# Linear attention and a gated feed-forward layer on one core: four more units and half a block in seven products, one more set turned by TensorE, a new opening

## The chip, the cores and the metric

The kernel runs on one core of one Trainium2 chip. The metric is the device time of one execution in microseconds, the median over several runs. Engines are named as in the profile: PE is TensorE (PEld its weight loads), DVE is VectorE, ACT is ScalarE, POOL is GpSimd, SP is SyncE, which here only issues DMAs.

## The reference

Attention with a decay for each head, in blocks of 64 positions, for 4 batches, 8 heads, 768 positions and 64 features; then a two-layer network with SiLU over 3072 tokens, 512 wide, 2048 inside. Inputs and outputs are float32.

```python
Dmask = np.where(rel >= 0, lam[:, None, None] ** rel[None, :, :], 0.0)      # rel = i - j in a block
lam_pow = lam[:, None, None] ** (pos[None, :, None] + 1)
for b in range(nb):
    qb, kb, vb = (q[:, :, sl], k[:, :, sl], v[:, :, sl])
    intra = np.einsum('bhic,bhjc->bhij', qb, kb) * Dmask[None]
    intra = np.einsum('bhij,bhjd->bhid', intra, vb)
    inter = np.einsum('bhid,bhde->bhie', qb * lam_pow[None], kv_state)
    out[:, :, sl] = intra + inter
    kb_dec = kb * lam[:, None, None] ** (block - 1 - pos[None, :, None])
    kv_state = lam_block[None, :, None, None] * kv_state + np.einsum('bhsd,bhse->bhde', kb_dec, vb)
x = attn_out.transpose(0, 2, 1, 3).reshape(3072, 512)
h = x @ w_in                     # 512 x 2048
out = (h / (1 + np.exp(-h))) @ w_out   # 2048 x 512
```

## The kernel before

**Units, sets, groups.** A unit is 128 positions of one batch, (n, b), with n = 0 to 5 and b = 0 to 3: 24 units, numbered in the order in which they are finished. The attention is done for sets of two units: sets 0 to 3 are blocks 0 and 1 of one batch each (units 0 to 7, "paired", functions `prepare_2`, `first_2`, `second_2`), sets 4 to 11 are two batches of one block n = 2 to 5. Each set loads q, k and v with SP's queue, casts and scales them to bf16 (`kq`, `vd`), turns k and q (`kqT`), makes scores (`st_ps`), masks them on DVE (`st`), makes the state's increment (`d_ps`), the new state (`xf`, and as blocks `xe` in bf16) and the output x, which is copied as `xt`. Sets below `TURNED` (5) are turned by PE transposes with four copies out of PSUM, the others by one DMA transpose on SP's queue.

**The first product.** Its tokens come in groups: groups 0 to 3 are the paired sets (256 tokens), groups 4 to 7 the blocks n = 2 to 5 (512 tokens; "block 4" is n = 4, group 6). `product1` multiplies w_in by xt in plain matmuls (four for each of the 16 rows of features, L905) and ACT applies SiLU to give g (L917). The last group goes through `product1_spared`: h is taken as a 2 x 2 matrix of blocks, and each of four passes `jp` makes four feature rows with seven block products (L1023, 28 matmuls of 256 columns in place of 16 of 512). It needs four sums of w_in (`S1` to `S4`, `sums_of_w_in`), four of xt (`T1` to `T4`), copies of partial results (`keep`) and sums (`total_of`).

**The second product.** `product2_plain` handles one unit with 16 matmuls of 512 columns (L940). Units from number `PLAIN` (8) on go four at a time through `product2`: seven products of 16 matmuls of 256 columns (L1153), with sums of g made by DVE (16 for four units, written as `s` or over `g`), sums of w_out (`sums_of_w_out`, the last over w_out itself once all plain units are done), kept products (`m`) and results added on DVE (`osb`). The last four units are done in two halves.

**The order.** Nothing is issued in the order of the program text. Each step is a task with a key (its rank), costs by engine, what it depends on, and the buffers that it takes; class `Planner` runs through time with these costs, a model of the DMA queues (`SMALL`, `LARGE` and so on, `FIRST`, `LAST`) and a slower PE at the start (`SLOW`), gives each engine the ready task with the lowest key, chooses the engine where there are several, and writes out the order. On the chip each engine then runs its list in that order. A task's key in the set's steps is `s`, which is the unit's rank less a lead, plus or minus a little. Early on, the planner puts PE matmuls without use ("ones", L1236) where PE would be idle.

The loads of the opening follow `SEQUENCE`: set 0, w_in's first part once set 0's v has landed, set 1, and so on; "s2@1.2" holds set 2's loads on SP until set 1's v has landed, by a small DMA that reads it (`held`, L439).

Of the kernel before, what the change touches and what calls it, by code (L numbers as in the profile page):

```python
# [216 lines left out]
def kernel(  # L217
# [27 lines left out]
    FRESH, TURNED, ALONE, LEAD = 4, 5, 6, 6.5  # L245
# [3 lines left out]
    BY_POOL, IN_BY_POOL, PLAIN, SPARED = (), (), 8, 1  # L249
# [4 lines left out]
    SCORED, SOON, VD_ON, HALVED = (0, 1), 3, {"DVE": 0.7}, 0  # L254
    EAGER, CALM, ON = 8.0, 1.0, 6.0
# [94 lines left out]


# [16 lines left out]
    def load_set(key, si):  # L368
        n, b = sets[si][0]
        nb = 2  # L370
        rs = [Buf("rb") if si >= CASTING and i == 0 else None if si >= CASTING and i == 1 else Buf("ra" if si in (0, 3) else "rb")
              for i in range(3)]
        ts = []
        x = [t[b, :, 0:2 * U, :].rearrange("h (p e) d -> p h (e d)", e=2) if n < PAIRED else
             t[b:b + 2, :, n * U:n * U + U, :].rearrange("b h s d -> s (b h) d") for t in (k, q, v)]

        def go(e, i):
            if n < PAIRED:
                tile_of(rs[i], [128, H, 2, 64], F32, "raw")
                nc.sync.dma_start(out=rs[i].tile.rearrange("p h e d -> p h (e d)"), in_=x[i])  # L380
            elif si >= CASTING and i < 2:
                tl = tile_of(rs[0], [128, 2, 2, NP, 2, 64], BF16, "kq")
                nc.gpsimd.dma_start(out=tl[:, i].rearrange("p b m h d -> p (b m h) d"), in_=x[i])
            else:
                nc.sync.dma_start(out=tile_of(rs[i], [128, 2 * H, 64], F32, "raw"), in_=x[i])

        for i in (1, 0, 2) if si in QUERIES else range(3):
            if si >= CASTING and i < 2:
                t = pool_task(add((key, i), {"POOL": 0.8}, lambda e, i=i: go(e, i), bufs=[rs[0]], nbytes=0.524, kind=CAST,
                                  prior=pool_last[-1:] + raw[si - 1][1][2], late=2.0))  # L390
                ts.append([t])
# [10 lines left out]
    def load_w(key, what, j, part):  # L402
        def go(e):
# [3 lines left out]
            else:  # L407
# [4 lines left out]
                          HALF if part else LARGE, prior=pool_last[-1:], late=1.0))  # L412
# [7 lines left out]
    for m, x in enumerate(SEQUENCE.split() + [f"s{i}" for i in range(len(sets))]):  # L420
# [59 lines left out]
    def prepare_2(o, rs, lk, lq, lv):  # L480
# [5 lines left out]
        def cast(e, i, a):  # L486
            src = rs[i].tile[:, :, a, :].rearrange("p (m h) d -> p m h d", h=2)
            if i:
# [5 lines left out]
        o.ck = [[add((s - (2.95 if i and o.si in SCALED else 1.0), i), {"DVE": 0.7} if i else {"DVE": 0.45, "ACT": 0.63}, lambda e, i=i, a=a: cast(e, i, a),  # L494
# [28 lines left out]
    def first_2(o):  # L523
# [26 lines left out]
        def blocks(xe, i, src, t, buf):  # L550
# [5 lines left out]
            return [add((s - 0.9, 5), {"POOL": 0.5, "ACT": 0.42}, lambda e, r=r: go(e, r), deps=[t], bufs=[xe, buf])  # L556
# [9 lines left out]
        def rest():  # L566
# [6 lines left out]
            t2 = add((s - 0.9, 5), {"DVE": 0.42}, lambda e: tt(e, xf_of(), y.tile, rate, AL.mult), deps=[t1], bufs=[y, xf_n])  # L573
# [5 lines left out]
        deps = [t for t in o.turned]  # L579
        o.masked = []  # L580
        for g in range(2):
# [9 lines left out]
            ts = add((s - 0.5, g), {"PE": 0.4}, scores, deps=deps, bufs=st_ps[g] + [o.kqT])  # L591
# [42 lines left out]
    def prepare(si):  # L634
# [28 lines left out]
        def cast(e, j, i):  # L663
            src = rs[i].tile[:, j * H:j * H + H, :]
            dst = kq_of()[:, i, j].rearrange("p m h d -> p (m h) d")
            if i:
# [4 lines left out]
        ck = [[add((s - 1.0, i), {"DVE": 0.7} if i else {"DVE": 0.45, "ACT": 0.63}, lambda e, j=j, i=i: cast(e, j, i),  # L671
# [4 lines left out]
        def scale_v(e, j):  # L676
            tt(e, vd_of()[:, j], rs[2].tile[:, j * H:j * H + H, :], lam_v[:, :, None].to_broadcast([128, H, 64]), AL.mult)

        cv = [add((s - 0.8, 0), VD_ON, lambda e, j=j: scale_v(e, j),
# [114 lines left out]
    def after_first(o, t):  # L794
# [20 lines left out]
        def blocks(b, src, deps, bufs, i):  # L815
# [6 lines left out]
            return [add((s - 0.9, i), {"POOL": 0.25 + w / 1000, "ACT": 0.2 + w / 1200, "DVE": 0.1 + w / 1900}, lambda e, r=r: go(e, r),  # L822
# [65 lines left out]
    def product1(gi):  # L888
# [5 lines left out]
        for m0 in range(0, KO, 2 * per):  # L894
# [69 lines left out]
    def sums_of_w_in():  # L964
        bufs = {name: Buf("kq") if i else Buf("rb") for i, name in enumerate(("S1", "S2", "S3", "S4"))}
# [4 lines left out]

        every = [t for o in infos if rank[o.n, o.bs[0]] < SUMS_AFTER for t in o.cv] + [t for o in infos[:CASTING] for ts in o.ck for t in ts]

        def total(name, a, b, op, deps, on):
            done[name] = [add((on, 8), {"POOL": 2.4} if name in IN_BY_POOL else {"DVE": 0.7}, lambda e, ks=ks: tt(
                e, W[name]()[:, ks], W[a]()[:, ks], W[b]()[:, ks], op), deps=deps, bufs=[bufs[name]])
# [9 lines left out]
    def product1_spared(gi, wbufs, wdone):  # L985
# [5 lines left out]
        def X(name):  # L991
            i, r = {"B11": (0, lo), "B12": (0, hi), "B21": (1, lo), "B22": (1, hi), "T1": (0, hi)}.get(name, (0, lo))
            if name in ("T2", "T4"):
                return tile_of(two, [128, 2, 2, 256], BF16, "xsum")[:, int(name == "T4")]
            if name == "T3":
                return tile_of(one, [128, 2, 256], BF16, "xsum")
# [9 lines left out]
        total("T1", "B12", "B11", AL.subtract, done["T3"], [])  # L1006
        total("T4", "B21", "T2", AL.subtract, done["T2"], [two])
        for jp in range(4):
            P, R = Buf("bank"), Buf("bank")
            held = [P, R, Buf("sp")]  # L1010
# [24 lines left out]
            narrow = {"22": Buf("vd"), "12": Buf("st")}  # L1035
# [175 lines left out]
    for gi in range(len(groups) - SPARED):  # L1211
        product1(gi)
# [4 lines left out]
    if SPARED:  # L1217
        made = sums_of_w_in()
        for gi in range(len(groups) - SPARED, len(groups)):
            product1_spared(gi, *made)  # L1220
# [52 lines left out]
```

## Time and profile before

| | us |
|---|---|
| median of 3 runs (lowest, highest) | 204.46 (204.32, 205.02) |
| the profiled execution: its time | 204.46 |
| its span in the trace | 202.4 |
| mean granted PE clock | 0.997 |
| busy: PE, DVE, ACT, POOL | 188.1, 135.5, 114.2, 21.8 |

DMA engines are at 9 tenths or more from the second to the 27th of the 40 slices of the span; 27.27 MB are read from HBM and 6.29 MB written. An engine's row in the slices gives its busy share in tenths. In the groups of instructions, "x16 | 7.2, 447" means sixteen of them, 7.2 us busy, 447 ns each.

### The profile page before, as it was taken

How to read it: one execution, taken by the hardware profiler on the slowest of the kernel's cores; microseconds unless marked ns; L12 is line 12 of the kernel's file. 1: busy time of each engine (PE TensorE's matmuls, PEld its weight loads, DVE VectorE, ACT ScalarE, POOL GpSimd, SP SyncE). 2: the span in 40 equal slices, each digit the busy share in tenths (PEclk: the TensorE clock that was granted, in tenths of full speed). 3: DMA queues.
4: the chain of work that ended last, by engine and by line, in shares of the span. 5: the costliest groups of instructions: out<-in, count | busy, mean ns of one | idle time of the engine just before them, and what ended most of it. 6: DMA issues, size and time to landing. Idle time of an engine off the chain costs nothing.

```text
span 202.4 us, 5779 instructions
## 1 busy us (share of the span) xinstructions
PE 188.1 (93%) x2494; PEld 135.0 (67%) x2512; DVE 135.5 (67%) x269; ACT 114.2 (56%) x207; POOL 21.8 (11%) x48
## 2 busy tenths in 40 slices
PE   0588999999999999999999999999999999999992
PEld 0476788557678655544488746486676778888881
DVE  6499620595997950969999774999577553646511
ACT  3836666327567642357764394945656575685320
POOL 6093100310110100001011000110200000000000
PEclk9999999999999999999999999999999999999998
DMA  3999999999999989999999999948001111003313
GB/s 94 301 274 202 216 215 250 254 193 212 239 269 242 206 204 261 174 267 212 202 142 231 253 194 222 225 104 160 2 3 55 52 52 36 19 0 107 104 50 108
DMA packets 87067, 33.40 MB, mean 165 GB/s; under 512 B 65026, under 2 KB 86018, under 8 KB 87042
## 3 DMA queue, kind: packets, MB, share of 16 engines
q1 hardware_dynamic: 77154, 23.07, 57.0%
q0 software_dynamic: 4752, 4.19, 12.9%
q10 hardware_dynamic: 5136, 5.77, 8.9%
q8 instruction: 19, 0.31, 0.7%
q14 instruction: 6, 0.05, 0.1%
HBM read 27.27 MB, written 6.29 MB: 166 GB/s over the span
## 4 chain that ended last, share of the span: by engine, by line
PE 84%; DVE 6%; DMA 4%; ACT 3%; issue 1%; DVEq 0%; SPq 0%
PE h_ps L905 33%; PE o_ps L1153 22%; PE o_ps L940 14%; PE h_ps L1023 6%; DMA raw<-in_k_dram 3%; DVE st L349 2%; PE x_ps L767 2%; PE d_ps L727 1%; PE tr L513 1%; PE x_ps L759 1%; DVE vd L349 1%; PE st_ps L737 1%; DMA out_dram<-osb 1%; ACT xt L342 1%; DVE kqT L344 1%
## 5 line engine op out<-in xcount | busy, mean ns | idle before, releaser
L905 PE MATMUL h_ps<-xt,w_in_bf 128*128 128x256 bf16 (+1 forms) x440 | 73.7, 317 | 0.7 <-ACT xt L342 0.3
L905 PEld LDWEIGHTS <-w_in_bf 128*128 128x128 bf16 x448 | 42.9, 98 | 24.9 <-issue 0.3
L917 ACT ACTIVATE g<-h_ps 128x512 bf16<-128x512 f32 x80 | 46.8, 595 | 20.9 <-PE h_ps L905 20.3
L940 PE MATMUL o_ps<-w_out_bf,g 128*128 128x512 bf16 x118 | 28.6, 379 | 0.8 <-issue 0.5
L1153 PEld LDWEIGHTS <-g 128*128 128x128 bf16 x256 | 25.0, 98 | 3.7
L349 DVE TENSOR_TENSOR st<-st_ps,tri 128x512 bf16<-128x512 f32 x32 | 20.3, 682 | 9.3 <-PE st_ps L737 9.3
L1153 PEld LDWEIGHTS <-s 128*128 128x128 bf16 x192 | 18.7, 98 | 2.8
L349 DVE TENSOR_TENSOR kq<-raw,lam_q 128x512 bf16<-128x512 f32 x24 | 16.3, 698 | 6.2 <-DMA raw<-in_q_dram 4.5
L940 PEld LDWEIGHTS <-g 128*128 128x128 bf16 x128 | 12.0, 98 | 12.0
L349 DVE TENSOR_TENSOR osb<-o_ps,m 128x512 f32<-128x512 f32 (+1 forms) x15 | 8.6, 581 | 13.4 <-ACT m L342 8.6
L342 ACT ACTIVATE xt<-x_ps 128x512 bf16<-128x512 f32 x16 | 9.7, 631 | 12.3 <-PE x_ps L767 9.2
L349 DVE TENSOR_TENSOR vd<-raw,lam_v 128x512 bf16<-128x512 f32 x24 | 15.7, 682 | 0.7 <-DMA raw<-in_v_dram 0.7
L1153 PE MATMUL o_ps<-w_out_bf,s 128*128 128x256 bf16 x128 | 15.3, 273 | 0.0
L1153 PE MATMUL o_ps<-wsum,g 128*128 128x256 bf16 x128 | 15.1, 273 | 0.0
L1153 PE MATMUL o_ps<-w_out_bf,g 128*128 128x256 bf16 x128 | 14.8, 273 | 0.0
L342 ACT ACTIVATE osb<-o_ps 128x512 f32<-128x512 f32 (+1 forms) x13 | 7.3, 564 | 12.7 <-PE o_ps L940 8.6
L349 DVE TENSOR_TENSOR s<-g 128x512 bf16<-128x512 bf16 x16 | 7.2, 447 | 10.8 <-ACT g L917 8.1
L342 ACT ACTIVATE m<-o_ps 128x512 f32<-128x512 f32 (+1 forms) x13 | 6.7, 515 | 13.1 <-PE o_ps L1153 12.9
L513 PE MATMUL tr<-ident,kq 128*128 128x128 bf16 x64 | 6.1, 241 | 7.7 <-DVE kq L349 7.5
L342 ACT ACTIVATE kq<-raw 128x512 bf16<-128x512 f32 x14 | 8.4, 624 | 4.5 <-DMA raw<-in_k_dram 4.0
L346 POOL CAST xe<-xf 64x256 bf16<-64x256 f32 (+1 forms) x8 | 5.1, 640 | 49.4 <-DVE xf L349 39.3
L513 PEld LDWEIGHTS <-kq 128*128 128x128 bf16 x64 | 4.6, 107 | 8.4 <-DVE kq L349 7.9
(90 smaller groups left out, 225.0 us busy)
## 6 DMA issues: line engine op xcount, KB each, us to landing
raw<-in_q_dram SPq DMA_DIRECT2D x12, 512.0 KB, 8.2
raw<-in_k_dram SPq DMA_DIRECT2D x12, 512.0 KB, 7.9
raw<-in_v_dram SPq DMA_DIRECT2D x12, 512.0 KB, 7.2
out_dram<-osb ACTq DMA_DIRECT2D x20, 256.0 KB, 4.2
w_out_bf<-in_moe_w_out_dram POOLq DMA_DIRECT2D x4, 512.0 KB, 14.9
w_in_bf<-in_moe_w_in_dram POOLq DMA_DIRECT2D x3, 512.0 KB, 11.7
w_in_bf<-in_moe_w_in_dram POOLq DMA_DIRECT2D x2, 256.0 KB, 8.2
out_dram<-osb ACTq DMA_DIRECT2D x4, 128.0 KB, 1.7
```

The lines of the kernel that those rows point to most:

```text
L342: nc.scalar.activation(o, i, AF.Copy)
L344: nc.vector.tensor_copy(o, i)
L346: nc.gpsimd.tensor_copy(o, i)
L349: (nc.vector if e == "DVE" else nc.gpsimd).tensor_tensor(o, a, b, op=op)
L513: nc.tensor.transpose(t[:, m, a], o.kq_of()[:, i, m, a], ident)
L727: nc.tensor.matmul(d_of(c)[rp, j, m, :], lhsT=o.kq_of()[r, 0, j, m, p, :], rhs=o.vd_of()[r, j, 2 * m + p, :], start=j == 0 and m == 0, sto ...
L767: nc.tensor.matmul(x_of(c)[:, j, m, :], lhsT=o.xe[c].tile[:, (bs[0] + j) % 2, m, :], rhs=o.kqT_of()[:, 1, j, m, halves[c]], start=False, s ...
L905: nc.tensor.matmul(t[:, j, :], lhsT=w_in_bf[:, ko, 128 * (m1 + j):128 * (m1 + j) + 128], rhs=xt[gi].tile[:, ko, :], start=(ko == 0), stop= ...
L917: nc.scalar.activation(t[:, half * per:half * per + per], bank.tile, AF.Silu)
L940: nc.tensor.matmul(t, lhsT=g.tile[:, j, 128 * gp:128 * gp + 128], rhs=w_out_bf[:, ko, :], start=(ko == 0), stop=(ko == KO - 1))
L1023: nc.tensor.matmul(t[:, j, :], lhsT=W[w]()[:, k2, f:f + 128], rhs=X(r)[:, k2, :], start=first and j == 0 and k2 == 0, stop=True, skip_grou ...
L1153: nc.tensor.matmul(t[:, i_, :], lhsT=src(j)[:, k2, 128 * r:128 * r + 128], rhs=W[w]()[:, 2 * j + k2, :], start=first and i_ == 0 and j == ...
```

## The change

- `PLAIN` 8 to 4: units 4 to 7 leave `product2_plain` and go through `product2`. `ON` 6 to 0: the sums of w_out get an earlier key.
- `MIXED = (0, 1)`: of group 6's four passes, two go through `product1_spared`, two stay in `product1`. Their copies use buffers of other pools (`kq`, `y`, `yf`). The sums of w_in lie in `rb` buffers but for S3, and come once the last load has been issued, no longer after the casts; T1 gets a place of its own.
- `TURNED` 5 to 6: set 5 is turned by PE.
- The held load ahead of set 2 counts 2.2 us in the plan instead of 0.15.
- In the paired sets: scores of one half wait for that half's turned pieces alone (`FINE`), the next state xf has a later key (`LAZY`), and its xe copies may run on ACT or DVE, not on POOL (`XE_2`).
- The planner's figures for DMA kinds and starts change.

```diff
-SMALL, WIDE, CAST, LARGE, HALF, TURN = (256, 17.5, 20.0), (512, 25.0, 28.0), (256, 14.0, 31.0), (2048, 88.0, 90.0), (1024, 58.0, 58.0), (1024, 50.0, 50.0)
+SMALL, WIDE, CAST, LARGE, HALF, TURN, PART = (256, 17.5, 20.0), (512, 25.0, 28.0), (256, 14.0, 31.0), (2048, 86.0, 86.0), (1024, 58.0, 58.0), (1024, 50.0, 50.0), (1024, 45.0, 45.0)
...
-    SLOW, SLOWER = 15.5, 1.8
+    SLOW, SLOWER = 14.0, 1.8
-    FIRST, LAST, AHEAD = {"SP": 1.9, "ACT": 1.15, "POOL": 2.5}, 1.0, 0.75
+    FIRST, LAST, AHEAD = {"SP": 1.7, "ACT": 1.15, "POOL": 3.0}, 1.0, 0.75
...
-    FRESH, TURNED, ALONE, LEAD = 4, 5, 6, 6.5
+    FRESH, TURNED, ALONE, LEAD = 4, 6, 6, 6.5
-    BY_POOL, IN_BY_POOL, PLAIN, SPARED = (), (), 8, 1
+    BY_POOL, PLAIN = (), 4
-    SCORED, SOON, VD_ON, HALVED = (0, 1), 3, {"DVE": 0.7}, 0
-    EAGER, CALM, ON = 8.0, 1.0, 6.0
+    SCORED, SOON, HALVED = (0, 1), 3, 0
+    LAZY, FINE, SAFE = 2.0, True, 0.3
+    XE_2, XE_B, XE_P = {"ACT": 0.42, "DVE": 0.35}, 0.1, True
+    MIXED, APART, KEPT = (0, 1), 1, "yf"
+    EAGER, CALM, ON = 8.0, 1.0, 0.0
...
         t = pool_task(add((key, 0), {"POOL": 0.8}, go, [], [], 0.5243 if part else 1.0486,
-                          HALF if part else LARGE, prior=pool_last[-1:], late=1.0))
+                          PART if part else LARGE, prior=pool_last[-1:], late=1.0))
...
-                held = [add((m - 100, -1), {"SP": 0.15}, lambda e, g=gates, tile=tile: nc.sync.dma_start(
+                held = [add((m - 100, -1), {"SP": 2.2}, lambda e, g=gates, tile=tile: nc.sync.dma_start(
...
-            return [add((s - 0.9, 5), {"POOL": 0.5, "ACT": 0.42}, lambda e, r=r: go(e, r), deps=[t], bufs=[xe, buf])
+            return [add((s - 0.9, 5), XE_2, lambda e, r=r: go(e, r), deps=[t], bufs=[xe, buf])
...
-            t2 = add((s - 0.9, 5), {"DVE": 0.42}, lambda e: tt(e, xf_of(), y.tile, rate, AL.mult), deps=[t1], bufs=[y, xf_n])
+            t2 = add((s + LAZY, 5), {"DVE": 0.42}, lambda e: tt(e, xf_of(), y.tile, rate, AL.mult), deps=[t1], bufs=[y, xf_n])
...
-            ts = add((s - 0.5, g), {"PE": 0.4}, scores, deps=deps, bufs=st_ps[g] + [o.kqT])
+            ts = add((s - 0.5, g), {"PE": 0.4}, scores, deps=o.turned[g::2] if FINE else o.turned, bufs=st_ps[g] + [o.kqT])
...
-    def product1(gi):
+    def product1(gi, tiles=None):
...
-        for m0 in range(0, KO, 2 * per):
+        for m0 in tiles or range(0, KO, 2 * per):
...
-        bufs = {name: Buf("kq") if i else Buf("rb") for i, name in enumerate(("S1", "S2", "S3", "S4"))}
+        bufs = {name: Buf("kq" if name == "S3" else "rb") for name in ("S1", "S2", "S3", "S4")}
...
-        every = [t for o in infos if rank[o.n, o.bs[0]] < SUMS_AFTER for t in o.cv] + [t for o in infos[:CASTING] for ts in o.ck for t in ts]
+        issued, casts = [sp_last[-1]], [t for ts in infos[-1].ck for t in ts]
...
-        total("S1", "A21", "A22", AL.add, loads + every, on)
+        total("S1", "A21", "A22", AL.add, loads, on)
-        total("S3", "A11", "A21", AL.subtract, loads + every, on + 0.2)
+        total("S3", "A11", "A21", AL.subtract, casts, on + 0.2)
...
-    def product1_spared(gi, wbufs, wdone):
+    def product1_spared(gi, wbufs, wdone, parts):
...
-        total("T1", "B12", "B11", AL.subtract, done["T3"], [])
+        total("T1", "B12", "B11", AL.subtract, xt_done[gi], [one])
-        for jp in range(4):
+        closing = gi == len(groups) - 1
+        for jp in parts:
...
-            narrow = {"22": Buf("vd"), "12": Buf("st")}
+            narrow = {"22": Buf("vd" if closing else "y"), "12": Buf("st" if closing else "y")}
-            b2, c2 = keep("kqT", [m6])
+            b2, c2 = keep("kqT" if closing else "kq", [m6])
-            b3, c3 = keep("xf", [m7])
+            b3, c3 = keep("xf" if closing else KEPT, [m7])
...
-    for gi in range(len(groups) - SPARED):
+    for gi in range(len(groups) - 2):
         product1(gi)
...
+    made = sums_of_w_in()
+    left = [j for j in range(4) if j not in MIXED]
+    if left:
+        product1(len(groups) - 2, [m for j in left for m in (2 * j, 2 * j + 8)])
+    if MIXED:
+        product1_spared(len(groups) - 2, *made, MIXED)
+    product1_spared(len(groups) - 1, *made, range(4))
```

More of the change, by code (lines that the diff above doesn't have):

```diff
@@ L349, in tt, with by_act, by_rate @@
         (nc.vector if e == "DVE" else nc.gpsimd).tensor_tensor(o, a, b, op=op)
+    def by_act(what, si, a):
+        return {"ACT": 1.7} if f"{what}{si}{a}" in ON_ACT else {"DVE": 0.7}
+    def by_rate(e, o, i, rate):
+        if e == "ACT":
+            nc.scalar.activation(o, i, AF.Copy, scale=rate)
+        else:
+            nc.gpsimd.tensor_scalar(o, i, rate, None, op0=AL.mult)
     gate = const.tile([128, 16], F32, name="gate")
@@ L487, in cast @@
             src = rs[i].tile[:, :, a, :].rearrange("p (m h) d -> p m h d", h=2)
-            if i:
+            if i and e != "DVE":
+                for h in range(H):
+                    by_rate(e, o.kq_of()[:, i, h // 2, a, h % 2], rs[i].tile[:, h, a], lam_q2[:, h, a:a + 1])
+            elif i:
                 rate = lam_q2[:, :, a].rearrange("p (m h) -> p m h", h=2)
@@ L665, in cast @@
             dst = kq_of()[:, i, j].rearrange("p m h d -> p (m h) d")
-            if i:
+            if i and e != "DVE":
+                for h in range(H):
+                    by_rate(e, dst[:, h], src[:, h], lam_q[:, h:h + 1])
+            elif i:
                 tt(e, dst, src, lam_q[:, :, None].to_broadcast([128, H, 64]), AL.mult)
@@ L676, in scale_v @@
         def scale_v(e, j):
+            if e != "DVE":
+                for h in range(H):
+                    by_rate(e, vd_of()[:, j, h], rs[2].tile[:, j * H + h], lam_v[:, h:h + 1])
+                return
             tt(e, vd_of()[:, j], rs[2].tile[:, j * H:j * H + H, :], lam_v[:, :, None].to_broadcast([128, H, 64]), AL.mult)
-        cv = [add((s - 0.8, 0), VD_ON, lambda e, j=j: scale_v(e, j),
+        cv = [add((s - 0.8, 0), by_act("v", si, j), lambda e, j=j: scale_v(e, j),
                   deps=lv, bufs=[rs[2], o.vd]) for j in range(nb)]
```

33 lines of the change are left out of this document (17 added, 16 removed).

## The prediction

> **What bounds the kernel now.** I read the page first (shares of the span, the 40 slices, the chain that ended last), then the busy time of each engine in stretches, then the waits of TensorE, then the chain in order of time.
>
> ```profile
> PE 188.1 (93%) x2494; PEld 135.0 (67%) x2512; DVE 135.5 (67%) x269; ACT 114.2 (56%) x207; POOL 21.8 (11%) x48
> PE   0588999999999999999999999999999999999992
> DVE  6499620595997950969999774999577553646511
> PE 84%; DVE 6%; DMA 4%; ACT 3%; issue 1%; DVEq 0%; SPq 0%
> ```
>
> From the fifth slice on TensorE stands at 9, and the chain that ended last is TensorE for 84% of the span. VectorE comes next and has full slices of its own. The stretches make it sharper:
>
> ```profile
> 18.70:24.40 5.70, 5.22 (x108) 4.12 (x102) 5.04 (x10) 3.22 (x7) 0.79 (x2) 1.00 1.23 214
> 24.40:195.20 170.80, 169.53 (x2168) 120.10 (x2186) 115.85 (x225) 99.47 (x175) 11.07 (x15) 1.00 0.78 160
> PE o_ps L940 <- issue: 0.5, 3, 0.2
> ```
>
> In a row the columns are the length, then busy time of PE, PEld, DVE, ACT and POOL, the granted clock, and DMA. From 24.4 to 195.2 us TensorE is idle for 170.80 - 169.53 = 1.27 us at full clock; the longest total among its waits there is the 0.5 us of the last row, without a releaser. So a microsecond taken out of TensorE's work there ends the kernel a microsecond earlier, unless it comes back as a wait. The time before 24.4 and the last 7.2 us (the final products' evacuation and store) are separate stages.
>
> **The change part by part.** TensorE's own work first.
>
> ```profile
> 60.65 0.45 PE tr L693 x8
> 74.08 1.73 PE o_ps L940 x8
> 150.63 1.73 PE h_ps L905 x8
> 172.90 1.75 PE h_ps L1023 x16
> 186.43 8.75 PE o_ps L1153 x80
> ```
>
> A plain matmul of 512 columns takes 1.73 / 8 = 0.216 us in either product, one of 256 columns 1.75 / 16 = 0.109 us in the first product and 8.75 / 80 = 0.109 us in the second.
>
> *Units 4 to 7, second product.* Removed: 4 units x 16 matmuls x 0.216 = 13.8 us. Added: seven products x 16 matmuls x 0.109 = 12.25 us. On the path: -1.55 us.
>
> *Half of block 4's first product.* Of four column pairs two go over. Removed: 2 x 16 x 0.216 = 6.9 us. Added: 2 x 28 x 0.109 = 6.1 us. On the path: -0.8 us.
>
> *Set 5 turned by TensorE.* Two groups of eight transposes at 0.45: +0.9 us.
>
> The sum on TensorE is -1.45 us. The weight loads are where this could fail, since a product of 256 columns needs a load for half the columns:
>
> ```profile
> L1153 PEld LDWEIGHTS <-g 128*128 128x128 bf16 x256 | 25.0, 98 | 3.7
> ```
>
> A load takes 98 ns and runs beside a matmul that needs 109, so it is just covered; the 80 matmuls in 8.75 us, loads included, show it. The Trainium skill (TensorE: Matmul & The Clock Gate, Back-to-back issue gap) speaks against this part: it says that in a stream of loads and matmuls both set the spacing, and that large matmuls pipeline, at about 131 ns for 512 columns. By that figure the 64 plain matmuls would take an estimated 8.4 us, less than the seven products' 12.25, and this part would lose 3.9 us. This trace doesn't agree: 512 columns take 216 ns each in row after row.
>
> Now what the other engines get for it.
>
> ```profile
> L349 DVE TENSOR_TENSOR s<-g 128x512 bf16<-128x512 bf16 x16 | 7.2, 447 | 10.8 <-ACT g L917 8.1 <-ACT g L1047 2.5
> L349 DVE TENSOR_TENSOR s<-s,g 128x512 bf16<-128x512 bf16 x16 | 6.7, 420 | 0.4
> L349 DVE TENSOR_TENSOR s<-g,s 128x512 bf16<-128x512 bf16 x16 | 6.6, 416 | 0.1
> L349 DVE TENSOR_TENSOR g<-g 128x512 bf16<-128x512 bf16 x16 | 7.5, 469 | 0.0
> L349 DVE TENSOR_TENSOR osb<-o_ps,m 128x512 f32<-128x512 f32 x9 | 6.2, 686 | 6.0 <-ACT m L342 3.9 <-PE o_ps L1153 2.2
> L342 ACT ACTIVATE m<-o_ps 128x512 f32<-128x512 f32 x8 | 4.8, 597 | 7.3 <-PE o_ps L1153 7.1
> L344 DVE COPY kqT<-tr 128x512 bf16<-128x512 bf16 x10 | 4.2, 424 | 7.5 <-PE tr L513 4.2 <-ACT kqT L342 3.1 <-PE tr L693 0.3
> 60.00:70.00 10.00, 8.25 (x16) 1.00 0.95 218
> 70.00:80.00 10.00, 3.37 (x6) 1.00 1.04 248
> 80.00:90.00 10.00, 7.78 (x14) 1.00 1.29 204
> 90.00:100.00 10.00, 9.18 (x18) 1.00 1.04 216
> ```
>
> For units 4 to 7 VectorE makes 16 sums of g: 4 x (0.447 + 0.420 + 0.416 + 0.469) = 7.0 us. It adds three results, 3 x 0.686 = 2.1 us, and copies two of set 5's four turned pieces, 2 x 0.424 = 0.85 us: together about 9.9 us. In the last four rows (VectorE's busy time alone) it is idle for 40 - 28.6 = 11.4 us between 60 and 100 us. So this fits, with little left. ScalarE gets three kept products at 0.597 and loses four plain evacuations of the same size, about nothing. The W_out sums keep their number; only the last of them no longer waits for eight units, but for four.
>
> ```profile
> L349 DVE TENSOR_TENSOR h<-h_ps,m 128x512 f32<-128x512 f32 x8 | 5.5, 687 | 4.5 <-ACT m L342 4.5
> 120.00:130.00 10.00, 5.71 (x12) 1.00 1.29 221
> 130.00:140.00 10.00, 10.00 (x22) 1.00 0.67 137
> 140.00:150.00 10.00, 7.56 (x13) 1.00 0.18 40
> ```
>
> For block 4's half, VectorE makes four sums of xt (I take 0.42 each, the bf16 sums above: 1.7 us) and four sums of h (2.75 us); ScalarE makes six copies (0.597 each by the row of m above, 3.6 us). VectorE's 23.3 of 30 us between 120 and 150 become about 27.7. The sums of W_in lie in this stretch before and after, now right behind the issue of the last load. This is the tightest place; it fits on the sum, and I add nothing for it.
>
> *The queues.* Set 5's DMA transpose leaves SP's queue and the DMA engines:
>
> ```profile
> kqT<-kq SPq DMA_TRANSPOSE x7, 6.5
> 69.48 3.39 SPq L702 DMA_TRANSPOSE kqT<-kq  x1
> 80.82 1.29 DVE L349 TENSOR_TENSOR st<-st_ps,tri 128x512 bf16<-128x512 f32 x2 [6.79 <-PE st_ps L737]
> ```
>
> The first of the seven holds SP's queue for 3.39 us and lands some 6.5 us after its issue; the loads queued behind it go out up to 3.4 us earlier, and set 5's attention can start some 7 us earlier than the 80.8 us at which VectorE gets its scores. Both are off the path now, since TensorE has other work meanwhile; they pay for the plain products of units 4 to 7, which were that other work. I cost them at nothing; with that cover gone they would show as idle TensorE at 75 to 80 us. The held load is the same single DMA in the same place on SP, ahead of set 2's loads; counting it at 2.2 us moves planned times only, so the order of other work, not a transfer: nothing.
>
> *The opening.* The scores of sets 0 to 3 wait for half of the turned pieces; the scaling that makes the next state (xf) and its two copies come later; xe copies go to ScalarE or VectorE instead of POOL.
>
> ```profile
> w_in_bf<-in_moe_w_in_dram POOLq DMA_DIRECT2D x1, 512.0 KB, 8.0
> 10.44 0.89 POOL L406 DMA_DIRECT2D w_in_bf<-in_moe_w_in_dram  x1 [0.36 <-issue]
> 18.72 1.05 PE L905 MATMUL h_ps<-xt,w_in_bf 128*128 128x256 bf16 x8
> 23.27 0.42 ACT L342 ACTIVATE xe<-xf 64x256 bf16<-64x256 f32 x1
> 23.59 0.72 ACT L342 ACTIVATE xt<-x_ps 128x512 bf16<-128x512 f32 x1
> 24.36 6.28 PE L905 MATMUL h_ps<-xt,w_in_bf 128*128 128x256 bf16 x56 [0.26 <-ACT xt L342]
> ```
>
> The first weights, issued at 10.44, land 8.0 us later, at 18.4; the first product starts at 18.72. Nothing in the change brings them earlier, so what the attention of set 0 gains before that is lost. From 18.7 to 24.4 TensorE is idle for only 5.70 - 5.22 = 0.48 us. If the xe copy at 23.27 is gone, xt starts 0.4 us earlier and the 0.26 us wait at 24.36 goes. Bounds: all of the 0.48 us and another 0.4 us of set 1's scores moved ahead of 18.7 on one side (-0.9), a worse order on the other (+0.3, about the 0.26 us wait again). I take -0.25, the wait that the trace shows.
>
> **Sum.** -1.45 - 0.25 = -1.7 us. The profiled execution took 204.46 us (span 202.4 and 2.06 around it), which is also the median of the three runs: 204.46 - 1.7 = **202.8 us**. The terms' spread: opening -0.9 to +0.3; the two places on VectorE up to +0.8 in small waits that don't add up to a stall; so 201.8 to 203.8 in this case.
>
> **Rivals.**
> *A, the opening gives more* than TensorE's idle time between 18.7 and 24.4, because the new plan also orders work better up to 46 us: -1.45 - 0.9 and up to 0.6 of the 1.27 us idle later: 201.5 us. For it: VectorE is almost full there (5.04 of 5.70). Against: TensorE is full too, and the weights' landing is unchanged. Chance 0.09.
> *B, no change.* The 1.45 us saved returns as waits of 0.1 to 0.4 us at the evacuations between the seven products, with VectorE near full at 60 to 70, 90 to 100 and 130 to 140 us: about 204.3 us. Chance 0.08.
> *C, slower: VectorE's sums come late at units 4 to 7.* The third product needs eight sums of group 3's features, 8 x 0.43 = 3.4 us. In front of them on VectorE can lie the casts of sets 5 and 6.
>
> ```profile
> L349 DVE TENSOR_TENSOR vd<-raw,lam_v 128x512 bf16<-128x512 f32 x24 | 15.7, 682 | 0.7 <-DMA raw<-in_v_dram 0.7
> 67.06 0.38 PE x_ps L759 x32
> 67.44 0.57 PE x_ps L767 x16
> ```
>
> Eight of them at 15.7 / 24 = 0.65 us make 5.2 us. Cover on TensorE: the first two products, which need no sum (3.5 us), set 5's transposes (0.9) and one burst of attention (0.38 + 0.57). 8.6 - 5.35 = 3.25 us of idle TensorE: 204.46 - 1.7 + 3.25 = 206.0 us. It decides when the uncovered wait is over 1.7 us. For it: plain products have no such wait, and VectorE is at 8.25 of 10 just before. Against: the 6.79 us in which VectorE had nothing to do, just there. Chance 0.12.
>
> *D, the weight loads are not covered* in the new places. If every second load of the 112 + 56 new matmuls stood alone, 84 x 0.098 = 8.2 us: 204.46 - 1.7 + 8.2 = 211.0 us; it decides from 17 loads on. Against: the 80 matmuls in 8.75 us hold all their loads. The rule cited above speaks on this side, since it makes the plain matmuls the cheaper ones. Chance 0.01.
>
> **How the numbers follow.** Forecast 0.70, A 0.09, B 0.08, C 0.12, D 0.01. A measurement here tells about 0.3%, 0.6 us, from no change. Faster by more: the forecast and A, 0.79, and a little of B, 0.01: 0.80. Within: the rest of B, 0.07. Slower by more: C and D, 0.13. The range from 201.2 to 205.0 takes in the forecast, A and B and the mild end of C; it leaves out the bulk of C, D and the ends, some 0.13.
>
> **What would show each step.** TensorE's busy sum falls by about 1.5 us outside the opening; 64 matmuls of 512 columns at L940 instead of 128, and 112 more of 256 columns in the second product at 0.109 us; six DMA transposes; 16 more transposes by TensorE; VectorE's busy time up by 12 to 15 us; idle TensorE between 24.4 and the last product still under 2 us. Wrong would be: matmuls of 256 columns over 0.115 us; TensorE waiting for VectorE's s near 70 to 85 us (C); idle TensorE near 40 to 46 us, where the next weights and set 2 arrive; or a first product later than 18.7 us.

## The result and the profile after

| | before | after |
|---|---|---|
| median, us (runs) | 204.74 (6) | 203.47 (6) |
| lowest, highest | 204.32, 205.16 | 203.12, 203.79 |
| the profiled execution: time, span | 204.46, 202.4 | 203.12, 201.4 |

The ratio is 0.994, 95% interval 0.992 to 0.996: 1.27 us faster, where 1.7 us was forecast. The kernel before was also timed beside each group of experiments, 17 to 31 executions at a time, with medians of 204.45 to 204.55 us; against these the gain is 1.0 to 1.1 us. The page of the changed kernel, its shares, slices and chain:

```profile
PE 188.0 (93%) x2608; PEld 143.0 (71%) x2608; DVE 144.8 (72%) x295; ACT 118.8 (59%) x223; POOL 22.2 (11%) x43
PE   0488999999999999999999999999999999999992
DVE  6498720585998999959997664999939872827511
PE 79%; DVE 12%; DMA 3%; ACT 3%; issue 1%; SPq 0%; DVEq 0%
```

TensorE's busy sum hardly moved (188.1 before), but the trace before lacks records: 2494 matmuls stand beside 2512 weight loads there, 2608 beside 2608 here. VectorE's sum rose by 9.3 us, and VectorE's share of the chain doubled from 6% to 12%. The stretches, columns as in the prediction; then the groups of instructions and the DMA issues that count what was changed (lines are renumbered: L933 is the old L905, L968 the old L940, L1181 the old L1153, L1051 the old L1023, L721 the old L693; L346, L348 and L353 are helpers, for ScalarE's copies, VectorE's copies and VectorE's sums and products):

```profile
18.70:24.40 5.70, 5.33 (x124) 4.26 (x115) 5.45 (x12) 4.25 (x10) 0.00 (x0) 1.00 1.23 214
24.40:195.20 170.80, 170.43 (x2283) 128.87 (x2284) 125.60 (x251) 103.46 (x191) 12.54 (x13) 1.00 0.74 157
60.00:80.00 20.00, 19.66 (x363) 15.25 (x362) 18.86 (x35) 14.32 (x27) 2.42 (x3) 1.00 1.12 217
120.00:150.00 30.00, 30.00 (x408) 21.86 (x407) 23.88 (x49) 16.69 (x30) 4.87 (x2) 1.00 0.48 109
```

```profile
L968 PE MATMUL o_ps<-w_out_bf,g 128*128 128x512 bf16 x64 | 15.8, 380 | 0.0
L721 PE MATMUL tr<-ident,kq 128*128 128x128 bf16 x32 | 2.3, 219 | 0.0
L353 DVE TENSOR_TENSOR s<-g 128x512 bf16<-128x512 bf16 x20 | 8.2, 416 | 1.5 <-ACT g L1075 1.4
```

```profile
kqT<-kq SPq DMA_TRANSPOSE x6, 5.7
```

All parts are there: 64 plain matmuls in the second product, 32 transposes by TensorE after the paired sets, four more sums of each kind, six DMA transposes. Between 24.4 and 195.2 us TensorE is idle for 0.37 us. The last group of matmuls shows what that is worth; its row in order of time starts at 196.75 us before and at 195.83 us after. Then come two rows of the chain after:

```profile
196.75 1.91 PE L1153 MATMUL o_ps<-w_out_bf,s 128*128 128x256 bf16 x16
```

```profile
195.83 1.91 PE L1181 MATMUL o_ps<-w_out_bf,s 128*128 128x256 bf16 x16
```

```profile
131.94 8.73 PE o_ps L1181 x80
146.48 3.06 PE h_ps L1051 x28
```

TensorE is done 0.92 us earlier, and a product still costs 0.109 us for 256 columns (8.73 / 80 and 3.06 / 28, the rows of the chain). The dense stretch starts at 24.43 us against 24.36. Counted by instructions TensorE has 1.45 us less to do, so 0.07 us came back at the start, and some 0.5 us in one place, here in order of time:

```profile
76.09 0.64 PE L795 MATMUL x_ps<-kqT,xe 128*128 128x64 bf16 x16
76.54 0.60 ACT L346 ACTIVATE xt<-x_ps 128x512 bf16<-128x512 f32 x1
76.57 1.04 PE L933 MATMUL h_ps<-xt,w_in_bf 128*128 128x256 bf16 x8
76.60 0.68 DVE L353 TENSOR_TENSOR xf<-y,lam_be 128x512 f32<-128x512 f32 x1
76.83 1.59 SPq L730 DMA_TRANSPOSE kqT<-kq  x1
77.20 0.68 DVE L348 CAST xt<-x_ps 128x512 bf16<-128x512 f32 x1
77.32 0.63 ACT L346 ACTIVATE xe<-xf 64x512 bf16<-64x512 f32 x1 [0.18 <-DVE xf L353]
77.94 0.33 PEld L933 LDWEIGHTS <-w_in_bf 128*128 128x128 bf16 x3 [0.61 <-DVE xt L348]
77.94 0.60 PE L933 MATMUL h_ps<-xt,w_in_bf 128*128 128x512 bf16 x2 [0.34 <-ACT xe L346]
```

The eight matmuls at 76.57 occupy the array for 8 x 0.109 = 0.87 us, until 77.44. The next matmuls, the first of block 2's first product, start at 77.94, 0.5 us later (the row counts 0.34 from the modelled end of the matmul before). The row puts the wait down to ScalarE's copy xe, but xe ends at 77.32 + 0.63 = 77.95 us, too late for it, and these matmuls don't read it; their weight load is marked with VectorE's xt. They need both copies of set 5's x; the second stands on VectorE behind the new state xf, starts at 77.20 and takes 0.68 us. VectorE is busy for 18.86 of the 20 us from 60 to 80 (11.62 before), and the chain runs through it for most of the time from 62.6 to 77.3 us (through ScalarE from 69.1 to 71.6).

The profiled executions differ by 0.34 us more outside the span (204.46 - 202.4 = 2.06 against 203.12 - 201.4 = 1.72). This is no accident of the pair. Time less span is 1.68 to 1.75 us in all six executions of the changed kernel and 2.01 to 2.16 us in the executions of the kernel before beside the experiments. So about 0.37 us of the gain is not in anything that the trace shows, and where it is from stays open. It differs between the experiments too (means of 2.0 to 2.1 us with units 4 to 7 plain, with set 5 turned by the DMA and with the plan's figures of before, 2.3 us with the new opening alone, 1.95 us with the sums earlier, 1.7 to 1.8 us in the others), so differences of 0.3 us between kernels can lie there.

### The profile page after: what moved, and what is told of

Its sections match the earlier page's. It is cut to its first block, busy times and chain, and to the rows that moved or that the text cites. A ratio compares the mean times of both kernels' runs of the same rounds, so it can differ in the third digit from the quotient of the medians.

```text
span 201.4 us, 6028 instructions
## 1 busy us (share of the span) xinstructions
PE 188.0 (93%) x2608; PEld 143.0 (71%) x2608; DVE 144.8 (72%) x295; ACT 118.8 (59%) x223; POOL 22.2 (11%) x43
## 4 chain that ended last, share of the span: by engine, by line
PE 79%; DVE 12%; DMA 3%; ACT 3%; issue 1%; SPq 0%; DVEq 0%
PE o_ps L1181 29%; PE h_ps L933 27%; PE h_ps L1051 9%; PE o_ps L968 6%; DVE st L353 4%; DMA raw<-in_k_dram 3%; PE x_ps L795 2%; PE tr L535 1%; PE d_ps L755 1%; DVE kq L353 1%; DVE y L353 1%; DVE vd L353 1%; DVE xe L348 1%; ACT kqT L346 1%; DVE xf L353 1%; PE st_ps L765 1%
## 5 line engine op out<-in xcount | busy, mean ns | idle before, releaser
L933 PE MATMUL h_ps<-xt,w_in_bf 128*128 128x256 bf16 (+1 forms) x416 | 67.0, 314 | 0.5 <-ACT xe L346 0.3
L933 PEld LDWEIGHTS <-w_in_bf 128*128 128x128 bf16 x416 | 39.8, 98 | 21.1 <-DVE xt L348 1.1
L945 ACT ACTIVATE g<-h_ps 128x512 bf16<-128x512 f32 x72 | 41.5, 594 | 16.3 <-PE h_ps L933 16.0
L1181 PEld LDWEIGHTS <-g 128*128 128x128 bf16 x320 | 31.2, 98 | 4.7
L1181 PEld LDWEIGHTS <-s 128*128 128x128 bf16 x240 | 23.4, 98 | 3.2
L346 ACT ACTIVATE m<-o_ps 128x512 f32<-128x512 f32 (+1 forms) x18 | 9.5, 525 | 23.4 <-PE o_ps L1181 23.4
L353 DVE TENSOR_TENSOR st<-st_ps,tri 128x512 bf16<-128x512 f32 x32 | 20.2, 680 | 3.2 <-PE st_ps L765 3.2
L353 DVE TENSOR_TENSOR osb<-o_ps,m 128x512 f32<-128x512 f32 (+1 forms) x18 | 10.7, 597 | 16.2 <-ACT m L346 9.2
L353 DVE TENSOR_TENSOR kq<-raw,lam_q 128x512 bf16<-128x512 f32 x24 | 16.2, 702 | 5.9 <-DMA raw<-in_q_dram 4.0
L1181 PE MATMUL o_ps<-w_out_bf,s 128*128 128x256 bf16 x160 | 19.1, 273 | 0.0
L1181 PE MATMUL o_ps<-wsum,g 128*128 128x256 bf16 x160 | 18.9, 273 | 0.0
L1181 PE MATMUL o_ps<-w_out_bf,g 128*128 128x256 bf16 x160 | 18.6, 273 | 0.0
L353 DVE TENSOR_TENSOR vd<-raw,lam_v 128x512 bf16<-128x512 f32 x24 | 15.9, 686 | 2.0 <-DMA raw<-in_v_dram 2.0
L968 PE MATMUL o_ps<-w_out_bf,g 128*128 128x512 bf16 x64 | 15.8, 380 | 0.0
L350 POOL CAST xe<-xf 64x512 bf16<-64x512 f32 x6 | 7.6, 1268 | 74.3 <-DVE xf L353 59.9
L346 ACT ACTIVATE xt<-x_ps 128x512 bf16<-128x512 f32 x18 | 11.2, 645 | 6.8 <-PE x_ps L795 5.9
L353 DVE TENSOR_TENSOR h<-h_ps,m 128x512 f32<-128x512 f32 x12 | 8.2, 687 | 9.0 <-ACT m L346 4.6
L346 ACT ACTIVATE kq<-raw 128x512 bf16<-128x512 f32 x17 | 10.2, 625 | 4.1 <-DMA raw<-in_k_dram 3.4
L1051 PEld LDWEIGHTS <-wsum 128*128 128x128 bf16 x96 | 9.4, 98 | 1.3
L346 ACT ACTIVATE kqT<-tr 128x512 bf16<-128x512 bf16 x14 | 7.9, 595 | 3.2 <-DVE kqT L348 2.6
```

What stands on the lines that cost most here:

```text
L346: nc.scalar.activation(o, i, AF.Copy)
L350: nc.gpsimd.tensor_copy(o, i)
L353: (nc.vector if e == "DVE" else nc.gpsimd).tensor_tensor(o, a, b, op=op)
L933: nc.tensor.matmul(t[:, j, :], lhsT=w_in_bf[:, ko, 128 * (m1 + j):128 * (m1 + j) + 128], rhs=xt[gi].tile[:, ko, :], start=(ko == 0), stop= ...
L945: nc.scalar.activation(t[:, half * per:half * per + per], bank.tile, AF.Silu)
L968: nc.tensor.matmul(t, lhsT=g.tile[:, j, 128 * gp:128 * gp + 128], rhs=w_out_bf[:, ko, :], start=(ko == 0), stop=(ko == KO - 1))
```

## The experiments

Theory: TensorE's work sets the time, so each part counts with its matmuls, and the wait at 77 us is the price of losing plain products as filling work. Rivals: VectorE sets the pace where it is full; or the new order, not the work, makes the gain. All kernels but one (set 5 turned twice) are planned anew by the changed kernel's planner, so a difference holds a part together with the order that comes without it. How much an order can do alone, the held load below shows: 1.5 us with no work changed. "Changed kernel" in numbers is 203.47 us, ratio 0.994.

**Units 4 to 7 plain again.**

```diff
-    BY_POOL, PLAIN = (), 4
+    BY_POOL, PLAIN = (), 8
-    EAGER, CALM, ON = 8.0, 1.0, 0.0
+    EAGER, CALM, ON = 8.0, 1.0, 6.0
```

> The changed kernel with units 4 to 7's second product plain again (PLAIN 8, and ON 6 with it). If TensorE's work is the bound, the seven products were worth 13.8 - 12.25 = 1.55 us, less the 0.5 us wait at 77 us that their lack of filling work left: 1.0 to 1.6 us slower than the changed kernel's 203.5, so 204.5 to 205.0, ratio to before 0.999 to 1.002, and the wait at 77 us is gone. If the sums on VectorE ate what the products saved (rival), no more than 0.3 us slower: ratio 0.994 to 0.996.

205.47 us, ratio 1.0055 (1.003 to 1.0081): 2.0 us slower than the changed kernel, more than the 1.0 to 1.6 us expected. VectorE's sums had not eaten what the products saved. The wait at 77 us is gone, but a longer one has come at 70.6 us, where VectorE's scaled v of set 5 is late:

```profile
70.44 0.32 PE L755 MATMUL d_ps<-vd,kq 64*64 64x64 bf16 x16
71.75 0.32 PE L755 MATMUL d_ps<-vd,kq 64*64 64x64 bf16 x16 [1.00 <-DVE vd L353]
```

The last group of matmuls starts 2.51 us later than the changed kernel's 195.83:

```profile
198.34 1.91 PE L1181 MATMUL o_ps<-w_out_bf,s 128*128 128x256 bf16 x16
```

That is 1.55 us of matmuls and about 1.0 us more of waits; half a microsecond is won back behind the last group (the span ends 5.06 us after its start, 5.57 in the changed kernel). By the medians the span is 1.65 us longer (203.4 against 201.75), and 0.34 us of the 2.0 lie outside it. What the order has in this, these runs don't separate.

**Block 4 plain, in three passes, in all four.**

```diff
-    MIXED, APART, KEPT = (0, 1), 1, "yf"
+    MIXED, APART, KEPT = (), 1, "yf"
```

The other two kernels have `(0, 1, 2)` and `(0, 1, 2, 3)` in this place.

> The changed kernel with all of block 4's first product plain (MIXED empty). If TensorE's work is the bound, 0.8 us slower than the changed kernel: 204.3, ratio to before 0.998. If VectorE's extra 4.5 us in its fullest stretch (120 to 150 us) had cost TensorE waits that ate the gain (rival), the same as the changed kernel, ratio 0.994, with less idle TensorE between 130 and 165 us.

> The changed kernel with three of block 4's four passes in seven products, between the change's two and the four that cost 0.6 us more than two. TensorE's work falls by 0.4 us against two passes. If the waits for copies at 149 to 157 us come only with the fourth pass: 203.1, ratio 0.992, and it beats the changed kernel. If they grow with each pass: 203.6 to 204.0, ratio 0.995 to 0.997. Chance of the first 0.45.

> The changed kernel with all four passes of block 4's first product in seven products. TensorE's work falls by another 2 x (3.46 - 3.05) = 0.8 us. If TensorE is the bound between 130 and 165 us: 202.7, ratio 0.990. If VectorE and ScalarE's copies (five more steps of 0.6 to 0.7 us for each pass, three or four of them on VectorE's side at most) hold TensorE up there: 203.5 to 204.5, ratio 0.994 to 0.999, with waits of TensorE for VectorE's h or ScalarE's m. Chance of the first 0.55.

Plain: 204.00 us, 0.9969 (0.9951 to 0.9987), 0.53 us slower than with two passes, of the 0.8 us counted. Three: 204.09 us, 0.998 (0.9963 to 0.9996). Four: 204.07 us, 0.9964 (0.9939 to 0.9988). So the first two passes gain, the next two don't, and neither of the versions with more passes beats the changed kernel. The intervals of two passes and of none (0.992 to 0.996 and 0.9951 to 0.9987) just overlap, so 0.53 us alone is hardly clear of noise; the trace of the plain version says it better:

```profile
196.48 1.91 PE L1181 MATMUL o_ps<-w_out_bf,s 128*128 128x256 bf16 x16
```

This last group starts 0.65 us later than the changed kernel's 195.83, and the dense stretch 0.16 us earlier (24.27 against 24.43), with no more idle time between (0.33 us from 24.4 to 195.2, 0.37 in the changed kernel): together the 0.8 us that were counted. With four, the waits of TensorE and the stretch from 150 to 160 us read:

```profile
PE h_ps L1051 <- ACT m L346: 0.6, 2, 0.3
```

```profile
150.00:160.00 10.00, 9.51 (x202) 7.62 (x202) 9.19 (x19) 8.24 (x16) 0.00 (x0) 1.00 0.01 2
```

VectorE and ScalarE are at 9.19 and 8.24 of 10 there, and TensorE waits for the kept products; from 24.4 to 195.2 us it is idle for 1.16 us. For three and for four passes the second expectation held, with three a little above its 204.0 us.

**Set 5: turned by the DMA again; turned by TensorE twice.**

```diff
-    FRESH, TURNED, ALONE, LEAD = 4, 6, 6, 6.5
+    FRESH, TURNED, ALONE, LEAD = 4, 5, 6, 6.5
```

```diff
                 def turn(e, j=j, bank=bank):
...
-                    for i in range(2):
+                    for i in [0, 1] * (2 if si == 5 else 1):
```

> The changed kernel with set 5 turned by the DMA again (TURNED 5). By TensorE's work alone it saves 16 transposes, 0.9 us: 202.6, ratio 0.990. Rival: set 5's attention then comes some 8 us later (its scores near 80 us instead of 72), and block 4's... the group of block 2 can start only behind it; TensorE has five of units 4 to 7's products (8.75 us) to put there, but they need sums from a full VectorE: 1 to 4 us of idle TensorE between 70 and 88 us, so 203.6 to 206, ratio 0.995 to 1.007. I hold the rival more likely, 0.65.

> The changed kernel, its order untouched, but set 5's 16 transposes are done twice over, with the same result. If TensorE's work is the bound at 66 to 69 us, the cost is the term itself, 0.9 us: 204.4, ratio 0.998. If VectorE is the bound between 62 and 78 us and TensorE's 0.5 us wait at 77 us is its slack, half of it is absorbed: about 0.4 us, 203.9, ratio 0.9965, and the wait at 77 us is shorter.

By DMA: 205.33 us, 1.004 (1.0025 to 1.0056), 1.9 us slower, of which 0.3 us lie outside the span, though it has 0.9 us less to do. The rival held. TensorE's matmuls with their waits:

```profile
74.73 0.60 PE L1181 MATMUL o_ps<-w_out_bf,s 128*128 128x256 bf16 x4
76.58 1.60 PE L1181 MATMUL o_ps<-w_out_bf,s 128*128 128x256 bf16 x12 [1.25 <-DVE s L353]
81.45 1.91 PE L1181 MATMUL o_ps<-wsum,g 128*128 128x256 bf16 x16 [0.69 <-ACT m L346]
84.86 1.91 PE L1181 MATMUL o_ps<-wsum,g 128*128 128x256 bf16 x16 [0.56 <-ACT m L346]
```

With set 5 late, the seven products themselves must fill, and each waits for the sum or the copy that it needs. The first of these waits, for VectorE's sum s, is that of rival C in the prediction, here in a kernel where the attention of set 5 does not stand between the products.

Twice: 203.48 us, 0.9946 (0.9926 to 0.9965). Sixteen transposes more cost 0.0 us by the medians; the two intervals together leave about 0.6 us open either way. The order was not planned anew, so the trace can be laid beside that of the changed kernel:

```profile
77.31 2.85 PE L933 MATMUL h_ps<-xt,w_in_bf 128*128 128x256 bf16 x15
196.16 1.91 PE L1181 MATMUL o_ps<-w_out_bf,s 128*128 128x256 bf16 x16
```

The eight matmuls that started at 76.57 start at 77.31, the wait behind them is filled, and the last group starts 0.33 us later (196.16, 195.83). So 0.74 of the 0.9 us arrive at these matmuls and 0.33 at the end; the wait took most of the difference. This fits the second expectation: VectorE is the bound between 62 and 78 us.

**The opening: of before; alone; and piece by piece.** The old opening in the changed kernel:

```diff
-SMALL, WIDE, CAST, LARGE, HALF, TURN, PART = (256, 17.5, 20.0), (512, 25.0, 28.0), (256, 14.0, 31.0), (2048, 86.0, 86.0), (1024, 58.0, 58.0), (1024, 50.0, 50.0), (1024, 45.0, 45.0)
+SMALL, WIDE, CAST, LARGE, HALF, TURN, PART = (256, 17.5, 20.0), (512, 25.0, 28.0), (256, 14.0, 31.0), (2048, 88.0, 90.0), (1024, 58.0, 58.0), (1024, 50.0, 50.0), (1024, 58.0, 58.0)
...
-    SLOW, SLOWER = 14.0, 1.8
+    SLOW, SLOWER = 15.5, 1.8
...
-    FIRST, LAST, AHEAD = {"SP": 1.7, "ACT": 1.15, "POOL": 3.0}, 1.0, 0.75
+    FIRST, LAST, AHEAD = {"SP": 1.9, "ACT": 1.15, "POOL": 2.5}, 1.0, 0.75
...
-    LAZY, FINE, SAFE = 2.0, True, 0.3
-    XE_2, XE_B, XE_P = {"ACT": 0.42, "DVE": 0.35}, 0.1, True
+    LAZY, FINE, SAFE = -0.9, False, 0.3
+    XE_2, XE_B, XE_P = {"POOL": 0.5, "ACT": 0.42}, 0.1, True
...
-                held = [add((m - 100, -1), {"SP": 2.2}, lambda e, g=gates, tile=tile: nc.sync.dma_start(
+                held = [add((m - 100, -1), {"SP": 0.15}, lambda e, g=gates, tile=tile: nc.sync.dma_start(
```

> The changed kernel with the opening of before: scores wait for all turned pieces, xf and its copies have their early key, xe copies on POOL or ScalarE, the held load counted at 0.15 us, and the planner's figures for DMA kinds, starts and slow TensorE as before. The trace shows the dense stretch of TensorE starting at 24.43 us against 24.36 before, so the new opening brought nothing: 203.5, ratio 0.994, with the start between 24.2 and 24.6. Rival: the new figures keep the later order tight, and without them waits of 0.5 to 1.5 us appear between 24 and 80 us: 204 to 205, ratio 0.997 to 1.001.

205.97 us, 1.0078 (1.0043 to 1.0112), 2.5 us slower: the rival, and more than it said. The start was not the matter (24.42 us). VectorE falls behind, x of set 5 is late, and TensorE waits twice at 77 to 80 us (in order of time; then the stretches with the columns as before, the granted clock third from the end):

```profile
78.66 0.39 PE L795 MATMUL x_ps<-kqT,xe 128*128 128x64 bf16 x8 [0.96 <-ACT xt L346]
79.73 6.16 PE L933 MATMUL h_ps<-xt,w_in_bf 128*128 128x512 bf16 x20 [0.69 <-ACT xt L346]
```

```profile
76.00:78.00 2.00, 1.69 (x49) 1.26 (x46) 2.00 (x4) 1.65 (x3) 0.00 (x0) 1.00 1.19 214
78.00:80.00 2.00, 0.66 (x10) 0.47 (x11) 1.94 (x5) 1.19 (x3) 0.00 (x0) 1.00 1.25 267
80.00:82.00 2.00, 2.00 (x7) 0.75 (x6) 2.00 (x4) 1.51 (x3) 0.91 (x1) 0.58 1.20 256
82.00:84.00 2.00, 2.00 (x6) 0.71 (x5) 2.00 (x8) 0.83 (x2) 0.00 (x0) 0.57 1.37 93
84.00:86.00 2.00, 2.00 (x12) 1.02 (x11) 2.00 (x7) 1.26 (x3) 0.00 (x0) 1.00 0.98 221
```

In this execution the granted clock falls to 0.58 behind the waits. Two of the seven runs are at 207.4 and 207.3 us, the other five at 205.8 to 206.2, so the fall is not what the median shows. That the median shows the waits is read from this one trace, which has both.

The new opening alone (the changed kernel with PLAIN 8, ON 6, MIXED empty and TURNED 5):

> The changed kernel with all three other parts taken back: units 4 to 7 and block 4 plain, set 5 turned by the DMA. What is left is the new opening with the plan's new figures. Theory: the opening takes nothing off TensorE's work or off the start of its dense stretch, so alone it gives the time of before, 204.2 to 204.8, ratio 0.999 to 1.002; the 1.0 to 2.5 us that its parts cost when taken back one at a time are the price of an order in which the plan and the chip disagree. Rival: it tightens the order by itself: 203.0 to 203.9, ratio 0.993 to 0.997.

204.66 us, 1.0009 (0.9985 to 1.0034). Alone it gives nothing, as the theory said: its median span is 202.35 us, that of the kernel before 202.4.

Piece by piece, each in the changed kernel: the held load at 0.15 us; the paired sets' tasks of before (XE_2, LAZY, FINE); the plan's figures of before. The expectation of the last one says that the held load counts 0.15 us there too; its edit leaves it at 2.2. So the three kernels each take back a separate piece, and the three pieces together are the old opening.

> The changed kernel with the held load counted at 0.15 us in the plan, as before, and nothing else of the old opening. The old opening as a whole cost 2.4 us, as waits of TensorE between 45 and 80 us. Theory: the old plan believes set 2 to be there 2 us too early, so VectorE and TensorE get an order of work that waits for loads: then most of the 2.4 us are here, 205 to 206, ratio 1.002 to 1.007. Rival: the tasks' order (xf, xe, scores by halves) or the DMA figures make it: 203.3 to 203.9 here, ratio 0.993 to 0.997. I give the theory 0.4.

> The changed kernel with the paired sets' tasks of before: xf and its copies early, xe copies on POOL or ScalarE, scores behind all turned pieces; the plan's figures and the held load stay new. If these tasks make the old opening's 2.4 us (POOL's copies of 0.4 to 0.8 us behind each other, and VectorE with an xf in front of xt): 205 to 206, ratio 1.002 to 1.007. If the figures or the held load make it: 203.3 to 203.9, ratio 0.993 to 0.997. Chance of the first 0.35.

> The changed kernel with the plan's old figures for DMA kinds, DMA starts and TensorE's slow beginning; the held load counts 0.15 us as before too, the tasks of the paired sets stay new. If the plan's figures make the old opening's 2.4 us: 205 to 206, ratio 1.002 to 1.007; if the tasks make it: 203.3 to 203.9, ratio 0.993 to 0.997. Together with the kernel that has only the held load of before, this separates the held load from the other figures.

205.01 us, 1.002 (1.0005 to 1.0035); 204.96 us, 1.0014 (0.9991 to 1.0037); 204.53 us, 0.9996 (0.998 to 1.0011). Against the changed kernel they cost 1.5, 1.5 and 1.1 us, 4.1 in sum where all together cost 2.5: they don't add up. None of the single causes that were set against each other holds alone. Each has its own wait. The first rows are those of the held load, then come the same places in the changed kernel, then the tasks and the figures:

```profile
28.24 1.29 DVE L353 TENSOR_TENSOR kq<-raw,lam_q 128x512 bf16<-128x512 f32 x2 [3.87 <-DMA raw<-in_q_dram]
28.99 0.23 PE L535 MATMUL tr<-ident,kq 128*128 128x128 bf16 x1 [0.89 <-DVE kq L353]
```

```profile
24.43 7.16 PE L933 MATMUL h_ps<-xt,w_in_bf 128*128 128x256 bf16 x64 [0.19 <-DVE xt L348]
28.37 1.29 DVE L353 TENSOR_TENSOR kq<-raw,lam_q 128x512 bf16<-128x512 f32 x2 [3.99 <-DMA raw<-in_q_dram]
31.43 0.61 PE L535 MATMUL tr<-ident,kq 128*128 128x128 bf16 x8
```

```profile
41.30 0.61 PE L535 MATMUL tr<-ident,kq 128*128 128x128 bf16 x8 [1.23 <-DVE st L353]
```

```profile
PE h_ps L933 <- ACT xt L346: 1.5, 2, 1.0
```

VectorE waits for the same q in both kernels, 3.87 and 3.99 us. What the held load changes is TensorE's order: in the changed kernel the transposes stand behind 64 matmuls and don't wait; the plan that expects set 2 two microseconds earlier puts them behind 32, and they wait for q, with the matmuls queued behind them. With the old tasks eight transposes wait 1.23 us for VectorE, which is at a set's masked products (st). With the old figures TensorE waits twice for ScalarE's xt, 0.96 us at 25.18, where the dense stretch starts, and 0.59 us at 79.33. Why the pieces don't add up stays open. A guess is that delays in the old plan partly cancelled (by the new figures its starts were too early for POOL and too late for SP), and no longer do when they are changed one at a time; no run shows it.

**The sums of units 4 to 7 earlier.**

```diff
-    EAGER, CALM, ON = 8.0, 1.0, 0.0
+    EAGER, CALM, ON = 8.0, 4.0, 0.0
```

> The changed kernel with the sums, copies and results of units 4 to 7's second product three units earlier in rank (CALM 4 in place of 1), so that VectorE takes them ahead of the casts of later sets. If the 0.5 us wait at 77 us is there because no third product is ready, it goes: 203.0, ratio 0.992. If what is put behind the sums (casts, masks of set 5) then comes late, another wait takes its place: 203.5 to 204.5. Chance of the first 0.4.

206.58 us, 1.0089 (1.0054 to 1.0125), 3.1 us slower: the second expectation, and worse. What VectorE does earlier for units 4 to 7 is missing later, and at 77 us nothing is won: there TensorE waits 0.64 us for VectorE's xt. Its waits between 60 and 130 us:

```profile
PE h_ps L933 <- DVE xt L348: 1.4, 2, 0.8
PE st_ps L765 <- issue: 1.3, 1, 1.3
PE o_ps L1181 <- ACT m L346: 0.7, 1, 0.7
```

The 1.3 us have no releaser; they lie within one group of scores, and what they are stays open.

## Why the prediction was right, and where not

*The bound.* TensorE's work from 24.4 us on was the right measure: 1.45 us less of it, 0.07 us lost at the start and 0.5 in the wait at 77 us leave 0.88, and the last group of matmuls starts 0.92 us earlier. The 1.27 us of idle time before was misread: 18 matmuls have no record in that trace, 10 of the 128 plain ones in the second product and 8 in the first product, and small "issue" gaps stand where records are missing. The kernel before had less idle time than the prediction thought: with its products and no record missing, the new opening alone has 0.23 us. With records missing, the busy sum doesn't show the fall of 1.5 us that the prediction named as a sign.

*Units 4 to 7, -1.55 us.* Right by the matmuls counted and their 0.109 us, unchanged. Taking it back costs 2.0 us, but in a new order, with a new wait and 0.34 us outside the span, so the run doesn't measure the term by itself. The Trainium skill's figure of 131 ns for 512 columns (TensorE: Matmul & The Clock Gate, Back-to-back issue gap) would have made going back to plain the faster way. It was the slower one, by 2.0 us.

*Block 4's half, -0.8 us.* Right: 0.53 us by the medians, 0.8 us by the two traces. VectorE stood at 23.9 of 30 us from 120 to 150, not at 27.7, because block 4's seven products come later than assumed: its four sums of h run at 149.8 to 157.1 us. That is where TensorE waits from the third pass on. In all, VectorE's busy time rose by 9.3 us, not by 12 to 15, and ScalarE's by 4.6.

*Set 5, +0.9 us.* The mechanism stood one paragraph below the sum: off the path, it pays for the plain products that used to fill. The sum still charged the full 0.9, though VectorE paces TensorE around 66 to 78 us. The doubled transposes cost 0.0 by the medians and 0.33 by the last matmul, with the wait filled. The idle TensorE "with that cover gone" at 75 to 80 us came as said when the DMA turned the set: 1.25 us at 76.58, and the kernel 1.9 us slower.

*The opening, -0.25 us.* This step failed. The prediction took it that the xe copy at 23.27 us would leave ScalarE, xt start 0.4 us earlier and the wait of 0.26 us go. In the changed kernel these rows read:

```profile
22.87 0.42 DVE L353 TENSOR_TENSOR xf<-y,lam_be 128x256 f32<-128x256 f32 x1
23.33 0.42 ACT L346 ACTIVATE xe<-xf 64x256 bf16<-64x256 f32 x1 [0.22 <-DVE xf L353]
23.33 0.29 DVE L348 CAST xe<-xf 64x256 bf16<-64x256 f32 x1
23.65 0.73 DVE L348 CAST xt<-x_ps 128x512 bf16<-128x512 f32 x1
23.65 0.72 ACT L346 ACTIVATE xt<-x_ps 128x512 bf16<-128x512 f32 x1
```

One xe copy is still on ScalarE; the other went from POOL to VectorE, in front of VectorE's xt, which started at 23.15 us before. So xt comes no earlier, the wait is 0.19 us for VectorE now, and the dense stretch starts 0.07 us later. Alone the new opening is worth nothing. "Moves planned times only ... nothing" for the held load was wrong as well: planned times are the order, and at 0.15 us the changed kernel takes 1.5 us longer.

*The wait at 77 us, 0.5 us.* Not in the sum, inside its spread of "up to +0.8". Its place is not rival C's: the third product runs at 84 us without a wait, and what was late is a copy of x behind xf. The estimate that VectorE's 9.9 us fit into 11.4 us was right in the mean (36.4 of 40 us from 60 to 100 after, 28.6 before) and blind to the order within: 7.2 of the 7.9 us that VectorE got more came between 60 and 80.

So the forecast's 1.7 us became 1.27: the -1.45 of work stands, the -0.25 of the opening didn't come, 0.5 came back as a wait, and 0.34 went away outside the span, which nothing foresaw and no view explains. Without that the gain had been some 0.9 us: that the time came so near the forecast is luck by this much.

## What to carry to other kernels

Where one engine is full, count an edit's work on it, but look for the engine that paces it in just that stretch: work added under such a wait costs little, and work removed there brings little. Trading matmuls for sums pays until the engines that make the sums and copies are full; here two passes of four were the limit. Filling work is worth keeping: with it gone, a late producer shows at once, and a plan's wrong delay that was harmless becomes a wait of a microsecond or two.

## What the runs showed of the hardware

The granted clock of TensorE fell to 0.57 to 0.58 from 80 to 84 us, after four microseconds (76 to 80) in which it was busy for 1.69 + 0.66 = 2.35 us; matmuls were running again when it fell. In rows of half a microsecond it is 0.50 from 80.5 to 83.5. The longest waits before it were of 1.0 and 0.7 us. It doesn't come each time: the two runs at 207.4 and 207.3 us have mean clocks of 0.992 and 0.986 and lie some 1.5 us above the other five. The trace shows the fall in the first, and for the second only its mean clock says so. The Trainium skill (TensorE: Matmul & The Clock Gate, What's actually happening) tells of a halved clock after an idle window of some 3.4 us. Here no idle stretch was half that long.
